# Query weights times the feature map: six heads as two row tiles of 60 rows in two PSUM banks

## The chip, the cores and the metric

The kernel runs on one core of one Trainium2 chip. The metric is the device time of one execution in microseconds; the figure quoted for a kernel is the median of several executions. TensorE multiplies matrices (a weight load and a matmul are records of their own, PEld and PE), VectorE (DVE), ScalarE (ACT) and GpSimd (POOL) work elementwise, and SyncE (SP) issues most of the DMA transfers.

## The reference

The model mixes a linear attention with learned feature maps and a SiLU feed-forward block on the same input `x` of 2048 rows by 640, with 32 heads of width 20. The change touches the query side of the attention:

```python
q, k, v = (x @ wqkv) split in 32 heads of 20
pq = einsum("bhsd,hdf->bhsf", q, w_phi)
phi_q = concat([softmax(pq), softmax(-pq)])
...
a = (phi_q (phi_k^T v) / (phi_q phi_k^T 1 + 1e-6)) @ wo
b = silu(x @ w1) @ w2
return g * a + (1 - g) * b          # g = sigmoid(sum(x * gate_w))
```

Since `pq = x @ (wq_h @ w_phi_h)` for each head, the kernel multiplies the query weights by the feature maps once, and then projects `x` with the products. Those weight products are what the change rewrites.

## The kernel before

All large products take operands split into a high and a low part, three passes for each (`PASSES`), with single-pass matmuls. The products of weights are exceptions: they take plain fp32 operands, and each of them becomes two passes on TensorE, with a weight load and a matmul record for each pass.

The work goes in stages: keys and values with the attention state, then the hidden layer of the feed-forward block by a fast scheme of seven products (`product`, line L652) for pairs of row tiles, then the queries and the attention's output, and at last the second feed-forward product (L1642). The change lies in the second half of the hidden layer, where `fuse(gi)` is put in between the products of the loop over `n` by a table `todo`: group 0 at one place of the pair `p = 1`, groups 1 and 2 in `p = 2`, 3 and 4 in `p = 3`, 5 in `p = 4`. The order on TensorE, VectorE, ScalarE and GpSimd is that of the code (`inorder`); on SP's queue a scheduler sets it.

One call of `fuse(gi)` handles a group of `GR` = 6 heads, so `GW` = 120 rows of the transposed query weights `wqT`; groups 0 to 4 are full (`NG` = 5), and group 5 has the two heads that are left, `REST` = 40 rows. It loads these rows (`wTq`), and for each of the `NC` = 5 chunks of 128 model columns multiplies the chunk (stationary, 120 rows by 128 columns) by the group's block-diagonal feature maps (moving, 120 rows by 120 columns, from `bd` in the tile `consts`). The first four chunks go to one PSUM bank (tiles `pwq..._0`), the fifth to another (`pwq..._4`). `split` then writes the high part with ScalarE and the rest with VectorE into `WQ` (tile `wq`), which is read much later, by the query projections (L519). `bank` hands out the eight PSUM banks in a fixed turn, to these products and to those of the hidden layer (tiles `p`, L652).

Other products that the prediction looks at are `pn` (L1331), which put 64 columns of weights alternately into the lower and the upper half of the array's columns.

Of the kernel before, what the change touches and what calls it, by code (L numbers as in the profile page):

```python
# [16 lines left out]
P = 128  # L17
S = 2048
D = 640
H = 32  # L20
DH = 20
F = 1728
NC = D // P
# [6 lines left out]
GR = 6  # L30
GW = GR * DH
NG = H // GR
REST = D - NG * GW
NJ = 2 * NG + 1
RC = 2 * REST
KH = 3
KD = KH * DH
# [3 lines left out]
HW = 64  # L41
C_MASK, C_EYE = 0, KF
C_ALL = C_EYE + 3 * HW
GAP = 2 * (HW - KD)
NPRE = 9
PB = (4, 5, 6, 7, 0, 1, 2, 3)
NQ = NF // 2
# [20 lines left out]
def mix_kernel(ctx: ExitStack, tc: tile.TileContext, xT, wqT, wkc, wkr, wv, bd, bdc, cst, wo, w1, w1r, w2, out):  # L68
    nc = tc.nc
# [36 lines left out]
    def raw(name):  # L106
        return rawp.tile([P, D + 2], F32, tag="raw", name=name, bufs=4)
# [10 lines left out]
    def big(name, home):  # L118
        t = big_tile(name, home)[:, : 2 * NC * D]
        return t.rearrange("p (s c d) -> p c s d", s=2, d=D)  # L120

    def wslot(name, dt=F32):
        return fq.tile([P, 2 * D], dt, tag="w", name=name, bufs=NPRE)

    def split(hi, lo, src, lo_eng="dve"):
        nc.scalar.copy(hi, src)  # L126
        eng = nc.vector if lo_eng == "dve" else nc.gpsimd
        eng.tensor_tensor(lo, src, hi.bitcast(F32), op=ALU.subtract)  # L128
# [27 lines left out]
    g = wp.tile([P, NT], F32, name="g")  # L156
# [73 lines left out]
        X["t", u].extend(t[:, :, k * 256 : (k + 1) * 256] for k in range(r.shape[1] // 256))  # L230

    def load_fused(gi, r):
        n = min(GW, D - gi * GW)
        nc.sync.dma_start(r[:n, :], wqT[gi * GW : gi * GW + n, :])

    def fused_mm(b, gi, r, c, out):
        n = min(GW, D - gi * GW)
        nc.tensor.matmul(out, r[:n, c * P : (c + 1) * P], b[:n, gi, :n], start=True, stop=True)  # L238

    def fused(b, hi, lo, gi, r, pp, c0, c1):  # L240

        n = min(GW, D - gi * GW)
        flat = pp if len(pp.shape) == 2 else pp.rearrange("p a b -> p (a b)")
        pv = flat.rearrange("p (b f) -> p b f", f=P)
        for c in range(c0, c1):
            fused_mm(b, gi, r, c, pv[:, c - c0, :n])
        cs = slice(gi * GW, gi * GW + n)
        split(hi[:, c0:c1, cs], lo[:, c0:c1, cs], pv[:, : c1 - c0, :n])

    def two(name):  # L250
        return wslot(name, F32R).rearrange("p (s d) -> p s d", s=2)
# [119 lines left out]
    for k in range(WARM):  # L371
# [4 lines left out]
            start=(k == 0),  # L376
            stop=(k == WARM - 1),
# [422 lines left out]
    with inorder(ACT, DVE, POOL, SP):  # L800
# [38 lines left out]
        t = NT - 1  # L839
# [3 lines left out]
        with inorder(PE):  # L843
# [23 lines left out]
            cs = [slice(c * 512, (c + 1) * 512) for c in range(2)]  # L867
# [79 lines left out]
    def bank(name):  # L947
        k = turns["bank"] = turns.get("bank", -1) + 1
        return ps.tile([P, 512], F32, tag=f"bank{(0, 2, 3, 4, 5, 6, 7, 1)[k % 8]}", name=name, bufs=1)
# [135 lines left out]
    kvb = {}  # L1085

    def load_b_consts():
        c = wp.tile([P, NC * WC], F32, tag="big0", name="consts", bufs=1)
        kvb["bd"] = c[:GW, : GR * P].rearrange("p (g f) -> p g f", f=P)
        kvb["cst"] = c[:, GR * P : GR * P + C_ALL - C_EYE]  # L1090
        nc.scalar.dma_start(kvb["bd"], bd)
        nc.scalar.dma_start(kvb["cst"], cst[:, C_EYE:])
        kvb["kvm"] = c[: KF + 1, 2 * D : 4 * D]
        nc.scalar.dma_start(kvb["kvm"], kv_d[: KF + 1])
# [76 lines left out]
    def fuse(gi):  # L1171
        rq = raw(f"wTq{gi}")
        load_fused(gi, rq[:, :D])
        for c0, c1 in ((0, 4), (4, NC)):
            fused(kvb["bd"], WQ[:, :, 0, :], WQ[:, :, 1, :], gi, rq, bank(f"pwq{gi}_{c0}"), c0, c1)

    def last_tables():
        kvb["zbc"] = wslot("zbc")
# [17 lines left out]
    with inorder(PE, DVE, ACT, POOL):  # L1196
# [5 lines left out]
        for n in range(1, NQ):  # L1202
            todo = plan(n)
            if n in (1, 3):
                i = n // 2
# [3 lines left out]
            if n in (2, 4):  # L1209
                i = n // 2 - 1  # L1210
# [9 lines left out]
        WQ = big("wq", 1)  # L1220
        for n in range(NQ, 2 * NQ):
            p = n - NQ
            todo = plan(n)
            if p == 0:
                todo[2] += [n_steps(1, 3)]
                todo[5] += [load_b_consts]
                todo[3] += [do(x_raw, 3, 0), do(x_raw, 3, 1)]
            if p == 1:
                todo[3] += [gates_out]
                todo[7] += [n_steps(1, 0), n_steps(1, 1)]  # L1230
            for gi in ((), (0,), (1, 2), (3, 4), (5,), ())[p]:
                todo[(4, 2)[gi % 2]] += [do(fuse, gi)]
            if p == NQ - 1:
                todo[0] += [last_tables]
                todo[1] += [lambda: w_odd_parts(kvb.pop("odd"))]
                todo[2] += [make_kvw, load_wo]
                todo[4] += [lambda: q_open(8, q_proj(8)), do(q_feat, 8)]
                todo[3] += [do(xb_load, 0)]
            h_pair(n, todo)
# [123 lines left out]
    def n_gaps(u):  # L1363
        nc.sync.dma_start(
            oTs[u][KD : KD + GAP].bitcast(F32),
            r_d[u].rearrange("(c k) s h t -> k s c (h t)", k=GAP),
        )
# [413 lines left out]
    with inorder(PE, DVE, ACT, POOL):  # L1781
# [36 lines left out]
        for b in range(1, NB):  # L1818
            acc = {k: o_acc(b, k) for k in (*KO, 0)}
            for f in range(NK):  # L1820
# [7 lines left out]
                for k in (*KO, 0) if f in (0, NC) else (1, 2, 3, 0, 6, 7, 5, 4):  # L1828
# [20 lines left out]
                    else:  # L1849
                        mh, h, with_ = {2: (0, 0, 1), 4: (1, 0, 7), 3: (0, 1, 5)}[k]  # L1850
# [90 lines left out]
```

## Time and profile before

| | |
|---|---|
| median of 3 runs | 721.98 us (721.87 to 722.0) |
| profiled execution | 721.97 us, span 720.2 us |
| TensorE busy | 714.1 us, 99% of the span, 4464 matmul records |
| VectorE, ScalarE, GpSimd busy | 530.5, 324.8, 311.4 us |
| weight products of the queries, L238 | 60 passes between 277.0 and 316.6 us |
| granted TensorE clock | 0.998 of full speed |

A row of the timeline gives the start and the length in microseconds from the span's start, the engine, the line, the operation, the tiles written and read, the rows and columns of the weights (as 120*128), the moving operand, and how many equal instructions follow each other. A length is that from the first one's start to the last one's end; a matmul's own length is longer than the step from one to the next, since they overlap. In square brackets stands the idle time of the engine ahead of the row and what ended it.

### The profile page before, as it was taken

What the parts mean: (1) busy time and instruction counts of PE and PEld (TensorE: products, weight loads), DVE (VectorE), ACT (ScalarE), POOL (GpSimd) and SP (SyncE); (2) the same over time, 40 slices, a digit from 0 to 9 for tenths busy, and PEclk for the clock granted to TensorE, in tenths of its full rate; (3) what the DMA queues carried; (4) which work ended last, traced back from release to release, by engine and by line L of the source; (5) the groups of instructions that cost most, each with busy time, mean ns of one, the idle gap of its engine ahead of it and who ended that gap; (6) DMA issues with size and microseconds to landing.
All of it is one profiled execution on the core that took longest, in us unless ns stands there. A gap on an engine that the chain in (4) does not pass through costs nothing.

```text
span 720.2 us, 12096 instructions
## 1 busy us (share of the span) xinstructions
PE 714.1 (99%) x4464; PEld 639.7 (89%) x4464; DVE 530.5 (74%) x981; ACT 324.8 (45%) x642; POOL 311.4 (43%) x223
## 2 busy tenths in 40 slices
PE   9999999999999999999999999999999999999997
PEld 7888888888888888888998999999898899999996
DVE  5677667679968996654678776767447998786975
ACT  5444344556645465535444634343424443243340
POOL 2378888894354623215557566644200000300302
PEclk9999999999999999999999999999999999999999
DMA  8232110200446487536100322011469528362622
GB/s 269 89 104 88 38 39 27 74 16 16 150 151 217 154 251 244 189 101 201 54 1 25 97 83 69 25 38 33 135 179 343 174 77 246 105 211 81 209 77 74
DMA packets 53967, 85.53 MB, mean 119 GB/s; under 512 B 5482, under 2 KB 24186, under 8 KB 53908
## 3 DMA queue, kind: packets, MB, share of 16 engines
q1 hardware_dynamic: 52213, 81.56, 35.4%
q10 hardware_dynamic: 1695, 3.20, 1.5%
q8 instruction: 35, 0.57, 0.3%
q14 instruction: 24, 0.20, 0.1%
HBM read 58.82 MB, written 25.92 MB: 118 GB/s over the span
## 4 chain that ended last, share of the span: by engine, by line
PE 94%; DVE 3%; ACT 1%; DMA 1%; POOL 0%; issue 0%; SPq 0%; DVEq 0%; ACTq 0%; POOLq 0%
PE acc L1642 25%; PE p L652 20%; PE kvp L560 17%; PE pa L1382 10%; PE pq L519 7%; PE pn L1331 2%; PE kv L530 2%; PE pT L1251 2%; PE kvp L600 2%; PE kvp L410 1%; PE kvq L410 1%; PE pwk L398 1%; PE pwq L238 1%; DVE eq L510 1%; ACT eq L1008 1%; DMA wvr<-wv 1%
## 5 line engine op out<-in xcount | busy, mean ns | idle before, releaser
L1642 PE MATMUL acc<-u,w 128*128 128x512 f32 (+1 forms) x600 | 115.6, 339 | 0.5 <-DVE acc_x L1839 0.5
L1642 PEld LDWEIGHTS acc<-u,w 128*128 128x128 f32 x600 | 95.4, 190 | 12.4 <-DVE acc_x L1839 1.0
L560 PE MATMUL kvp<-wh,xa 128*128 128x512 f32 (+1 forms) x420 | 91.6, 354 | 0.0
L1650 POOL TENSOR_TENSOR o_0l<-o_0l,y 128x512 f32<-128x512 f32 x3 | 3.9, 1291 | 183.1 <-DMA ur<-u_d 111.8
L560 PEld LDWEIGHTS kvp<-wh,xa 128*128 128x128 f32 x420 | 70.3, 188 | 10.2
L1382 PE MATMUL pa<-oT,wo 128*128 128x256 f32 x600 | 74.3, 283 | 0.0
L1382 PEld LDWEIGHTS pa<-oT,wo 128*128 128x128 f32 x600 | 72.3, 188 | 0.9 <-issue 0.7
L1022 POOL TENSOR_TENSOR ez<-eq,zbc 128x1280 f32<-128x1280 f32 x16 | 47.0, 2938 | 30.7 <-ACT eq L1008 28.8
L615 ACT ACTIVATE u<-p 128x512 f32<-128x512 f32 x47 | 28.1, 599 | 67.9 <-issue 34.5
L128 POOL TENSOR_TENSOR ph<-ek,ph 128x1280 fp32r<-128x1280 f32 x15 | 44.8, 2984 | 19.4 <-ACT ph L126 17.9
L1058 POOL TENSOR_TENSOR eq<-eq,sm 128x1280 f32<-128x1280 f32 x16 | 37.9, 2368 | 33.3 <-DVE sm L1052 29.9
L279 POOL TENSOR_TENSOR wt<-wr 128x256 f32<-128x256 f32 (+1 forms) x36 | 27.9, 775 | 51.7 <-DVE ws10b L282 10.6
L126 ACT CAST t<-ur 128x512 fp32r<-128x512 f32 x36 | 22.4, 621 | 60.5 <-DVE ur L282 58.5
L360 ACT CAST v<-kvp 128x8 fp32r<-128x8 f32 (+3 forms) x75 | 16.8, 270 | 69.4 <-PE kvp L560 63.8
L560 PE MATMUL kvp<-wl,xa 128*128 128x512 f32 (+1 forms) x210 | 47.1, 354 | 0.0
L128 DVE TENSOR_TENSOR u<-ur,u 128x512 fp32r<-128x512 f32 x52 | 38.3, 762 | 6.3 <-ACT u L126 6.3
L1642 PEld LDWEIGHTS acc<-t,s 128*128 128x128 f32 x324 | 40.9, 191 | 1.0
L1642 PE MATMUL acc<-t,s 128*128 128x256 f32 x324 | 41.7, 283 | 0.0
L560 PEld LDWEIGHTS kvp<-wl,xa 128*128 128x128 f32 x210 | 35.7, 189 | 5.5
L588 POOL TENSOR_TENSOR ek<-ek,st 128x1280 f32<-128x1280 f32 x15 | 36.1, 2404 | 9.0 <-ACT v L360 6.2
L519 PE MATMUL pq<-wq,xb 128*128 128x320 f32 x240 | 37.2, 312 | 0.0
L519 PE MATMUL pq<-wq,xn 128*128 128x320 f32 x240 | 36.8, 310 | 0.0
(467 smaller groups left out, 1652.4 us busy)
## 6 DMA issues: line engine op xcount, KB each, us to landing
u_d<-u SPq DMA_DIRECT2D x52, 256.0 KB
ur<-u_d SPq DMA_DIRECT2D x52, 256.0 KB
wr<-w SPq DMA_DIRECT2D x24, 320.0 KB
w2r<-w SPq DMA_DIRECT2D x13, 320.0 KB
y<-fb_d SPq DMA_DIRECT2D x8, 512.0 KB
xra<-xT SPq DMA_DIRECT2D x14, 256.0 KB
xr<-xT SPq DMA_DIRECT2D x14, 256.0 KB
fb_d<-pac SPq DMA_DIRECT2D x14, 256.0 KB
```

The source lines that it names most:

```text
L126: nc.scalar.copy(hi, src)
L128: eng.tensor_tensor(lo, src, hi.bitcast(F32), op=ALU.subtract)
L279: nc.gpsimd.tensor_tensor(o[k], x, y, op=op)
L519: nc.tensor.matmul(dst, xt[c][:, hx, :], w[:, c, hw, lo : lo + n], start=first, stop=(hx == 1 and c == NC - 1))
L560: nc.tensor.matmul(kv_cols(t, k, lo, hi), xt[c][:, hx, :], WKV[hw][k][:, c, lo:hi], start=(n == 0), stop=(n == 3 * NC - 1), skip_group_che ...
L588: nc.gpsimd.tensor_tensor(groups(e), groups(e), spread(st[:, 1, :]), op=ALU.mult)
L615: nc.scalar.activation(o, src, AF.Silu)
L652: nc.tensor.matmul(dst, W[n][w][:, hw, j * P : (j + 1) * P], x[:, hx, :], start=(i == 0), stop=(i == len(todo) - 1))
L1022: nc.gpsimd.tensor_tensor(ez, Q[t]["e"], kvb["zbc"], op=ALU.mult)
L1058: nc.gpsimd.tensor_tensor(groups(q["e"]), groups(q["e"]), spread(q["sm"][:, 2 * H : 4 * H]), op=ALU.mult)
L1382: nc.tensor.matmul(pa[:, a, :], kvb["wo"][:, c, hw, ds], o[:, ho, c, :], start=(k == 0), stop=(k == len(todo) - 1),)
L1642: nc.tensor.matmul(dst, lhs, rhs, start=(first and n == 0), stop=(last and n == len(todo) - 1), skip_group_check=True)
```

## The change

The 120 rows of a full group are laid out as two tiles of 60 rows, at rows 0 to 59 and 64 to 123 of 128 (`ROWS`, with four rows of zeros between, so `wqT` and `bd` grow), and each tile multiplies its three heads alone: 60 rows of weights by a moving block of 60 columns. The two tiles of a chunk follow each other in the code and write to two banks, tile 0 to `pwq..._0` and tile 1 to `pwq..._1`, five chunks of 60 columns in each. Group 5 keeps its five products of 40 rows and puts them in one bank. The copies of a full group become two of 5 x 60 columns per engine instead of 4 x 120 and 120; group 5 has one per engine instead of two.

```diff
+GP = HW + KD
+ROWS = ((0, KD), (HW, KD))
...
     def load_fused(gi, r):
-        n = min(GW, D - gi * GW)
-        nc.sync.dma_start(r[:n, :], wqT[gi * GW : gi * GW + n, :])
-
-    def fused_mm(b, gi, r, c, out):
-        n = min(GW, D - gi * GW)
-        nc.tensor.matmul(out, r[:n, c * P : (c + 1) * P], b[:n, gi, :n], start=True, stop=True)
-
-    def fused(b, hi, lo, gi, r, pp, c0, c1):
-
-        n = min(GW, D - gi * GW)
-        flat = pp if len(pp.shape) == 2 else pp.rearrange("p a b -> p (a b)")
-        pv = flat.rearrange("p (b f) -> p b f", f=P)
-        for c in range(c0, c1):
-            fused_mm(b, gi, r, c, pv[:, c - c0, :n])
-        cs = slice(gi * GW, gi * GW + n)
-        split(hi[:, c0:c1, cs], lo[:, c0:c1, cs], pv[:, : c1 - c0, :n])
+        n = GP if gi < NG else REST
+        nc.sync.dma_start(r[:n, :], wqT[gi * P : gi * P + n, :])
+
+    def fused(b, hi, lo, gi, r, banks):
+
+        views = [t[:, : NC * HW].rearrange("p (c f) -> p c f", f=HW) for t in banks]
+        tiles = ROWS if gi < NG else ((0, REST),)
+        for c in range(NC):
+            for v, (r0, w) in zip(views, tiles):
+                rows = slice(r0, r0 + w)
+                nc.tensor.matmul(v[:, c, :w], r[rows, c * P : (c + 1) * P], b[rows, gi, :w], start=True, stop=True)
+        for a, (v, (_, w)) in enumerate(zip(views, tiles)):
+            cs = slice(gi * GW + a * KD, gi * GW + a * KD + w)
+            split(hi[:, :, cs], lo[:, :, cs], v[:, :, :w])
...
-        for c0, c1 in ((0, 4), (4, NC)):
-            fused(kvb["bd"], WQ[:, :, 0, :], WQ[:, :, 1, :], gi, rq, bank(f"pwq{gi}_{c0}"), c0, c1)
+        fused(kvb["bd"], WQ[:, :, 0, :], WQ[:, :, 1, :], gi, rq, [bank(f"pwq{gi}_{k}") for k in range(2)])
```

On TensorE, at group 0, between products of the hidden layer (`p`, from the raw and summed inputs `xn`, `xt`), the order before is this:

```order
L652 MATMUL p_4_2864<-xt_2017,ws7b 128x512 x2
L652 MATMUL p_4_2864<-xn_4_2582,ws7b 128x512
L238 MATMUL pwq_0_2885<-consts,wTq_2883 128x120 x4
L238 MATMUL pwq_4_2892<-consts,wTq_2883 128x120
L652 MATMUL p_5_2896<-xt_2014,ws7b 128x512 x2
```

In its place the changed kernel has the following, of whose ten rows of L245 the first two stand here; the other eight take the two banks in turn likewise.

```order
L652 MATMUL p_4_2864<-xt_2017,ws7b 128x512 x2
L652 MATMUL p_4_2864<-xn_4_2582,ws7b 128x512
L245 MATMUL pwq_0_2885<-consts,wTq_2883 128x60
L245 MATMUL pwq_1_2886<-consts,wTq_2883 128x60
...
L652 MATMUL p_5_2901<-xt_2014,ws7b 128x512 x2
```

Five products became ten, at the same place; the second bank is written by the second product and no longer by the fifth.

On SP's queue, around the loads of groups 2 to 5 (`wTq2` to `wTq5`), stores of the hidden layer `u_d` and weight loads `wr` stand in this order before:

```order
L234 DMA wTq2_3020<-wqT 120x640
L234 DMA wTq3_3100<-wqT 120x640
L234 DMA wTq4_3152<-wqT 120x640
L616 DMA u_d_109<-u2_3_2878 128x512
L616 DMA u_d_109<-u3_3_2910 128x512
L616 DMA u_d_109<-u3_2_2925 128x512
L1132 DMA g_d_108<-gT_2930 16x128
L262 DMA wr10_2965<-w1 128x640
L263 DMA wr10_2965<-w1 128x640
L234 DMA wTq5_3229<-wqT 40x640
L616 DMA u_d_109<-u2_4_2961 128x512
```

and in the changed kernel in this:

```order
L236 DMA wTq2_3030<-wqT 124x640
L236 DMA wTq3_3115<-wqT 124x640
L616 DMA u_d_109<-u2_3_2878 128x512
L236 DMA wTq4_3172<-wqT 124x640
L616 DMA u_d_109<-u3_3_2915 128x512
L616 DMA u_d_109<-u3_2_2930 128x512
L1132 DMA g_d_108<-gT_2935 16x128
L262 DMA wr10_2970<-w1 128x640
L263 DMA wr10_2970<-w1 128x640
L616 DMA u_d_109<-u2_4_2966 128x512
L236 DMA wTq5_3254<-wqT 40x640
```

The loads of groups 4 and 5 each moved behind one store, and three later loads on the queue (`w1l`, `w1r` and the first of `wo`) did so too.

More of the change, by code (lines that the diff above doesn't have):

```diff
@@ L1088, in load_b_consts @@
         c = wp.tile([P, NC * WC], F32, tag="big0", name="consts", bufs=1)
-        kvb["bd"] = c[:GW, : GR * P].rearrange("p (g f) -> p g f", f=P)
+        kvb["bd"] = c[:GP, : GR * P].rearrange("p (g f) -> p g f", f=P)
         kvb["cst"] = c[:, GR * P : GR * P + C_ALL - C_EYE]
@@ L1872 @@
     dt = x.dtype
-    bd = np.zeros((GW, GR, P), dt)
+    bd = np.zeros((GP, GR, P), dt)
     for h in range(H):
-        r, c = (h % GR) * DH, h // GR
-        bd[r : r + DH, c, r : r + DH] = w_phi[h]
+        r, j = ROWS[h % GR // KH][0] + h % KH * DH, h % KH * DH
+        bd[r : r + DH, h // GR, j : j + DH] = w_phi[h]
     bdc = np.zeros((GW, GR * DH + GR), dt)
@@ L1889, with spaced @@
     cst = blocks.astype(dt)
+    def spaced(a):
+        out = np.zeros((*a.shape[:-2], P, a.shape[-1]), dt)
+        for i, (r0, w) in enumerate(ROWS):
+            out[..., r0 : r0 + w, :] = a[..., i * KD : i * KD + w, :]
+        return out
     def tiles(a, n):
@@ L1906 @@
         "xT": x[0].T,
-        "wqT": wqkv[:, :D].T,
+        "wqT": np.concatenate([spaced(wqkv[:, : NG * GW].T.reshape(NG, GW, D)).reshape(NG * P, D), wqkv[:, NG * GW : D].T]),
         "wkc": rows(wqkv[:, D : D + NG * GW].reshape(NC, P, NG, GW).transpose(0, 3, 2, 1).reshape(NC, GW, NG * P), P),
```

## The prediction

> **What bounds the kernel now.** I read the page's busy times and its chain first, then the list of what TensorE waited for, then line L238, which the change replaces, and at last the timeline around single groups.
>
> ```profile
> PE 714.1 (99%) x4464; PEld 639.7 (89%) x4464; DVE 530.5 (74%) x981; ACT 324.8 (45%) x642; POOL 311.4 (43%) x223
> PE 94%; DVE 3%; ACT 1%; DMA 1%; POOL 0%; issue 0%; SPq 0%; DVEq 0%; ACTq 0%; POOLq 0%
> PE warm L372 <- DVE ones L172: 1.1, 1, 1.1
> PE acc L1642 <- DVE acc_x L1839: 0.5, 1, 0.5
> PE kvp L410 <- ACT wh L126: 0.2, 1, 0.2
> ```
>
> TensorE is busy 99% of the span and makes 94% of the chain that ended last. The last three rows are all its waits: 1.8 us in sum, at the kernel's start and end. Nothing behind the changed stage waits for an engine that runs on its own clock, so a microsecond more or less of TensorE there should reach the end one for one.
>
> ```profile
> L238 PEld LDWEIGHTS pwq<-consts,wTq x60: 182/192/193, 277.0 to 316.3; 120*128 120x128 f32 x50, 40*128 40x128 f32 x10
> L238 PE MATMUL pwq<-consts,wTq x60: 266/275/300, 277.3 to 316.3; 120*128 120x120 f32 x50, 40*128 40x40 f32 x10
> 306.29 0.40 PE L652 MATMUL p<-xn,ws9b 128*128 128x512 f32 x1
> 306.52 1.27 PE L238 MATMUL pwq<-consts,wTq 120*128 120x120 f32 x10
> 307.56 0.71 PE L652 MATMUL p<-xt,ws9b 128*128 128x512 f32 x2
> 308.10 0.40 PE L652 MATMUL p<-xn,ws9b 128*128 128x512 f32 x1
> 280.47 2.21 PE L652 MATMUL p<-xn,ws7d 128*128 128x512 f32 x9
> 314.49 0.84 PE L652 MATMUL p<-xn,ws10a 128*128 128x512 f32 x3
> 315.26 1.30 PE L238 MATMUL pwq<-consts,wTq 40*128 40x40 f32 x10
> 316.49 0.50 PE L652 MATMUL p<-xt,ws10c 128*128 128x512 f32 x1
> 316.83 0.63 PE L652 MATMUL p<-xt,ws10c 128*128 128x512 f32 x2
> 306.29 1.32 PEld L238 LDWEIGHTS pwq<-consts,wTq 120*128 120x128 f32 x10
> 315.26 1.19 PEld L238 LDWEIGHTS pwq<-consts,wTq 40*128 40x128 f32 x10 [0.35 <-issue]
> ```
>
> A product of these weights is two passes, each with a load of 128 columns. That makes 10 passes per group: five groups with 120 rows and 120 moving columns, and a sixth with 40 and 40, which the change leaves as it is on TensorE. In group 4, ten passes of 0.275 us overlap into 1.27 us, so one starts every (1.27 - 0.275) / 9 = 0.111 us. In the sixth, with a third of the rows and a third of the moving columns, the loads start every (1.19 - 0.19) / 9 = 0.111 us. The step is the same, so neither moving columns nor rows set it. What the two have in common is the load of 128 columns: this stage is bound by its weight loads.
>
> **What a change of the array's shape costs.** The sixth group is the nearest row for the new form, since 60 rows like 40 occupy half of the array's rows, between neighbours of 128. A 128x512 pass of the neighbours takes (2.21 - 0.39) / 8 = 0.227 us. From 306.29 to 308.10 lie the starts of group 4 and three neighbours: 1.81 - 0.68 = 1.13 us for ten passes. From 314.49 to 316.83 lie those of the sixth group and four neighbours: 2.34 - 0.91 = 1.43 us for ten passes at the same step. The half-height group costs 0.30 us more, around its passes and not in them: its first load starts with its first pass at 315.26, while group 4's runs under the matmul before, 0.23 us ahead of its pass, and the neighbour behind starts late likewise. The Trainium skill has this as a rule (TensorEngine Tiling (Array Packing), Key Properties): a change of the tiling mode drains TensorE, a change of tile alone does not. It gives no time; by it, too, a group pays on the way in and on the way out, not between its passes, and the sum below stays.
>
> **Two tiles at once.** No row shows two row tiles side by side. The nearest are the products pn, which alternate between two halves of the array's columns:
>
> ```profile
> L1331 PEld LDWEIGHTS pn<-fT,kvw x192: 132/137/139, 373.6 to 520.2; 120*64 120x64 f32 x160, 80*64 80x64 f32 x32
> 373.62 0.14 PEld L1331 LDWEIGHTS pn<-fT,kvw 120*64 120x64 f32 x2 [0.19 <-issue]
> 373.62 2.60 PE L1331 MATMUL pn<-fT,kvw 120*64 120x256 f32 x24
> 373.62 0.44 PE L1331 MATMUL pn<-fT,kvw 120*64 120x256 f32 x2
> 373.89 0.60 PE L1331 MATMUL pn<-fT,kvw 120*64 120x256 f32 x4
> ```
>
> Two loads of 0.13 to 0.14 us fill 0.14 us together, and two matmuls fill 0.44: in column tiles loads and passes start in pairs, within 0.01 us. I take row tiles to do the same.
>
> **The change, part by part.**
> - Passes: a group goes from 10 passes to 20 (10 products of 60 rows, two passes each), alternately in the upper and the lower half. Each half has 10 loads of 128 columns. If the halves load side by side, as pn's do, a group takes 10 steps of 0.111 us as before: 0. If they load one after the other, 10 steps are added: +1.11 us. Below nothing is bounded by the step itself: loads at half the step would give -0.56. I take 0, because pn is the only row with two tiles. The second half trails by 0.01 us.
> - The moving columns halve (120 to 60): 0, because the load's step covers them already in the sixth group.
> - Shape: five groups now change it on the way in and out, each between 128-row neighbours: 5 x 0.30 = +1.5 us, and 5 x 0.01 for the trailing half. The other end of this term is 0, if the neighbours hide the drain.
> - The second bank is needed at the second product, not at the fifth, so some 0.9 us earlier. Banks turn in eights.
>
> ```profile
> 298.77 0.59 ACT L687 COPY q<-p 128x512 f32<-128x512 f32 x1
> 307.50 0.60 ACT L615 ACTIVATE u<-p 128x512 f32<-128x512 f32 x1 [3.45 <-issue]
> 308.00 0.72 ACT L126 CAST wq<-pwq 128x480 fp32r<-128x480 f32 x2
> 286.07 1.27 PE L238 MATMUL pwq<-consts,wTq 120*128 120x120 f32 x10
> 283.11 0.85 DVE L128 TENSOR_TENSOR wq<-pwq,wq 128x480 fp32r<-128x480 f32 x2 [1.57 <-ACT wq L126]
> 308.58 0.85 DVE L128 TENSOR_TENSOR wq<-pwq,wq 128x480 fp32r<-128x480 f32 x2 [0.37 <-ACT wq L126]
> 279.56 1.40 SPq L234 DMA_DIRECT2D wTq<-wqT  x3
> 282.65 4.67 SPq L616 DMA_DIRECT2D u_d<-u  x3
> 288.82 0.32 SPq L234 DMA_DIRECT2D wTq<-wqT  x1
> 289.23 0.33 SPq L616 DMA_DIRECT2D u_d<-u  x1
> ```
>
>   For group 4 (306.52) ScalarE's copy at 298.77 frees that bank, 7 us ahead. The tightest is group 1 at 286.07, freed by VectorE's pair that ends at 283.96, 2.1 us ahead. No new stall: 0.
> - Copies: 480 and 120 elements become 300 and 300, still two instructions and 600 elements on each engine (0.72 and 0.85 us together); the sixth group loses one on each. ScalarE casts group 4 at 308.00, behind its activation and after the last pass started (307.5), so passes that end 0.3 us later may move it by some 0.1 us. TensorE has no wait here to lengthen, and the banks have 2 us: 0.
> - DMA: the five loads carry 124 rows, not 120, and `bd` too. On SP's queue the loads of groups 4 and 5 move behind one store u_d each. Group 4's is the last of three at 279.56, and would go after the store at 282.65 for use at 306.5; group 5's goes from 288.82 to behind the store at 289.23, for use at 315.26. What follows on the queue (the odd weights, wo) moves by one store likewise. 20 us of cover: 0. Without it a late load would stop TensorE for as long as it is late.
>
> Sum: +1.5 + 0.05 = +1.55 us. The profiled execution took 721.97 us (span 720.2, 1.8 outside), which stands at the median of 721.98. Forecast 723.5 us, +0.2%. The measurement tells about 0.2%, or 1.44 us, from no change: the bound lies at 723.42, so the forecast is barely above it.
>
> **Rivals.**
> - The halves take turns. If row tiles share the path of the weights, ten loads are added per group: 5 x (1.11 + 0.30) = +7.1 us, 729.0. For it: L238's step is a pure load step, and nothing shows row tiles loading together. Against it: pn. A weaker form is a limit on issue: 24 loads and 24 matmuls of pn take (2.60 - 0.27) us, 0.049 us each, and 40 instructions at that pace would need 1.95 us: 5 x (0.84 + 0.30) = +5.7, 727.7. But pn is paced by its 256 columns, so the row doesn't show a limit.
> - In between, passes side by side but started strictly in the program's order: each product then costs 0.111 + 0.007 us, +0.07 a group, 723.9. I count it with the forecast.
> - Faster, or not slower: the step halves, because a half-height load ends sooner when two share the array. Then 5 x (-0.56 + 0.30) = -1.3 us, 720.7. It decides once the step falls below 0.081 us, where the loads save what the shape costs. Against it: 40 rows load at 0.111. The Trainium skill (TensorEngine Tiling (Array Packing), Theoretical Speedup) promises up to twofold for a contraction of at most 64, which would be this case; it is a speedup of streaming, and the sixth group's rows show loads in its place.
> - The shape costs nothing, or is regained: if the cost of the sixth group belongs to its 40 rows, or a later stall is filled, the time is 722.0 to 722.5. Against it: the waits list has no stall before the end.
>
> **How the numbers follow.** Forecast with its ordered variant 0.72 (723.0 to 724.2 by itself), turns or issue 0.14, halved step 0.05, no cost 0.09. The forecast and no cost hold 0.81: range 721.9 to 724.6, with the other two left out. Of the forecast I give 0.62 to times above 723.42, because the ordered variant and the trailing half only add. Slower: 0.72 x 0.62 + 0.14 = 0.59. Faster by over 0.2% needs the halved step at its lower end: 0.03. Within 0.2%: 0.38.
>
> **What would show it.** The new line's loads start in pairs, every 0.111 us, and its ten products fill 1.1 us. The gap to the 128x512 passes on both sides grows by 0.30 us per group, as the sixth group's is now. TensorE's list of waits stays at 1.8 us. If the loads follow each other at 0.111 us, the first rival holds; if a group's passes fill 0.6 us, the faster one. A new wait of TensorE for pwq's banks or for wTq would prove my zeros wrong.

## The result, and the profile after

The changed kernel takes 731.93 us (median of 4 runs, 731.7 to 734.16) where the kernel before takes 721.99 (4 runs, 721.87 to 722.08): a ratio of 1.0144, interval 1.0132 to 1.0157, slower by 9.94 us. The forecast was +1.55 and its range ended at 724.6. The profiled execution of the changed kernel took 731.70 us (span 729.9), 0.2 us under its median.

The page's busy times, the chain's shares by engine, and the list of what TensorE waited for (waits in us: sum, times, longest), all of the kernel after:

```profile
PE 718.5 (98%) x4514; PEld 641.9 (88%) x4514; DVE 529.0 (72%) x980; ACT 324.4 (44%) x641; POOL 310.5 (43%) x223
PE 82%; DVE 8%; DMA 4%; ACT 3%; issue 3%; POOL 0%; DVEq 0%; ACTq 0%; POOLq 0%
PE pwq L245 <- ACT ws8b L288: 5.5, 1, 5.5
PE warm L372 <- DVE ones L174: 1.1, 1, 1.1
...
```

One row is new: TensorE waits 5.5 us, once, at the changed line. The chain has DMA in it, 4% against 1%. The other 4.4 us show in TensorE's busy time, which grew from 714.1 to 718.5. The timeline of TensorE places both, first at group 0 and then at group 4, which the prediction showed for the kernel before:

```profile
277.06 0.39 PE L652 MATMUL p<-xn,ws7b 128*128 128x512 f32 x1
282.99 2.40 PE L245 MATMUL pwq<-consts,wTq 60*128 60x60 f32 x20 [5.55 <-ACT ws8b L288]
...
286.76 1.05 PE L652 MATMUL p<-xt,ws7b 128*128 128x512 f32 x2
287.62 0.63 PE L652 MATMUL p<-xn,ws7b 128*128 128x512 f32 x1
...
294.65 1.33 PE L245 MATMUL pwq<-consts,wTq 60*128 60x60 f32 x20
...
315.79 0.39 PE L652 MATMUL p<-xn,ws9b 128*128 128x512 f32 x1
316.11 1.33 PE L245 MATMUL pwq<-consts,wTq 60*128 60x60 f32 x20
317.37 0.73 PE L652 MATMUL p<-xt,ws9b 128*128 128x512 f32 x2
317.94 0.40 PE L652 MATMUL p<-xn,ws9b 128*128 128x512 f32 x1
```

Group 4 is as forecast: twenty passes in 1.33 us, and from 315.79 to 317.94 lie 2.15 us, less 0.68 for three neighbours 1.47, where the kernel before had 1.13. Group 0 is another thing. TensorE idles 5.55 us ahead of it, its twenty passes then take 2.40 us, and two neighbours of 128x512 behind it take 287.62 - 286.76 = 0.86 us, nearly twice their 0.45. The next rows are windows. Each gives its start and end, its length, the busy microseconds and the instructions of TensorE's matmuls, its weight loads, VectorE, ScalarE and GpSimd, then the granted clock as a share of full speed, the busy share of the DMA engines, and GB/s:

```profile
277.00:283.00 6.00, 0.45 (x3) 0.06 (x3) 4.09 (x7) 3.41 (x7) 0.00 (x0) 0.89 0.75 222
283.00:285.00 2.00, 2.00 (x20) 2.00 (x20) 1.82 (x4) 0.00 (x0) 0.38 (x1) 0.50 0.25 96
285.00:289.00 4.00, 4.00 (x14) 3.13 (x13) 0.84 (x2) 1.62 (x4) 2.93 (x5) 0.56 0.41 150
289.00:300.00 11.00, 11.00 (x64) 8.87 (x63) 5.55 (x10) 4.87 (x11) 0.00 (x0) 1.00 0.57 201
```

The clock falls to half at 281.7, still in the idle time, and is back at 288.5, so TensorE works 5.5 us at half its clock. That is the larger part of the growth of its busy time.

What was group 0 waiting for? The waits list names ScalarE's cast `ws8b`, which the product doesn't read: the list names what ended last by the profile. The changed line's own group says more, for it also holds the waiting instructions of TensorE's sequencer (their shortest, median and longest in ns, then the first and last start). The rows of ScalarE's queue give the issue of `bd`, before and after:

```profile
L245 PEldq EVENT_SEMAPHORE  x6: 51/51/9709, 273.2 to 320.9; - x6
270.84 0.34 ACTq L1091 DMA_DIRECT2D consts<-bd  x1
271.56 0.27 ACTq L1091 DMA_DIRECT2D consts<-bd  x1
```

The longest wait, 9.71 us from 273.2, ends at 282.9. It waits for two semaphores, those of group 0's `wTq` and of `bd`, and the events of these semaphores in the trace show what happened at 282.9. A transfer reports in parts:

```
transfer            rows  issued   parts  landed
before     bd       120   270.84   15     274.06 to 274.88
after      bd       124   271.56    4     281.75 to 282.90
before     wTq0     120   263.93   15     268.33 to 270.35
after      wTq0     124   263.62    4     270.33 to 270.78
before     u_d      128   268.89   16     270.80 to 272.14
after      u_d      128   268.58   16     12 by 270.65, 4 at 275.29 to 275.75
```

With 120 rows a transfer is made of 15 parts, with 128 rows of 16, and with 124 rows, which are 4 x 31, of 4. So `bd` (372 KB) took 11.3 us instead of 4.0, and it is used at 277.3. The Trainium skill states the rule (DMA: Bandwidth & Descriptors, "Why a DMA increments its semaphore by 16 and not by 1"): a transfer runs on the largest number of engines up to 16 that divides the slowest dimension on both its sides, and on SP's and ScalarE's queues on the lowest-numbered ones. The trace agrees on the number, 15, 4 and 16; the last two rows also fit the second half, since a store on 16 engines waited 4.6 us longer for just four of its parts. Which engines these are the trace doesn't name.

### The profile page after: what moved, and what is told of

The parts are those of the page before. It is cut to its first block, busy times and chain, and to the rows that moved or that the text cites. A ratio compares the mean times of both kernels' runs of the same rounds, so it can differ in the third digit from the quotient of the medians.

```text
span 729.9 us, 12193 instructions
## 1 busy us (share of the span) xinstructions
PE 718.5 (98%) x4514; PEld 641.9 (88%) x4514; DVE 529.0 (72%) x980; ACT 324.4 (44%) x641; POOL 310.5 (43%) x223
## 4 chain that ended last, share of the span: by engine, by line
PE 82%; DVE 8%; DMA 4%; ACT 3%; issue 3%; POOL 0%; DVEq 0%; ACTq 0%; POOLq 0%
PE acc L1641 25%; PE kvp L560 17%; PE pa L1381 10%; PE p L652 8%; PE pq L519 7%; DMA u_d<-u 4%; PE pn L1330 2%; PE kv L530 2%; PE pT L1250 2%; PE kvp L600 2%; PE kvp L410 1%; PE kvq L410 1%; PE pwq L245 1%; PE pwk L398 1%; DVE p L657 1%
```

## The experiments

Each is run beside the kernel before, which took 722.12 us (9 runs, 721.83 to 722.47) in the first four and 722.15 (22 runs, 721.93 to 723.01) in the others.

**All rows loaded.** The changed kernel, with 128 rows instead of 124 in both transfers:

```diff
-        n = GP if gi < NG else REST
+        n = P if gi < NG else REST
...
-        kvb["bd"] = c[:GP, : GR * P].rearrange("p (g f) -> p g f", f=P)
+        kvb["bd"] = c[:, : GR * P].rearrange("p (g f) -> p g f", f=P)
...
-    bd = np.zeros((GP, GR, P), dt)
+    bd = np.zeros((P, GR, P), dt)
```

> The changed kernel, but the loads of bd and of the five full groups' wTq carry 128 rows instead of 124 (four more rows of zeros); row tiles, banks and the order on every queue stay. Theory (the row count of the transfers): in the changed kernel each 124-row transfer posts its completion in 4 parts where a 120-row one posts 15, so it runs on fewer DMA engines, and bd lands at 282.9 us where TensorE wants it at 277.3. With 128 rows bd should land within some 4 us of its issue, TensorE should not idle at group 0, and what is left is the shape cost of groups 1 to 4 of the changed kernel, 1.475 - 1.137 = 0.34 us, five times: +1.7 us, 723.7 us. Rival 1 (the row tiles themselves, or their first use, stall group 0): 731 to 732 us as before. Rival 2 (SP's order, in which two loads and three later ones moved behind a store): also 731 to 732 us, since that order is kept.

Measured: 724.63 us (723.83 to 725.01), ratio 1.0032 (1.0021 to 1.0044). That is 0.9 us more than the theory's 723.7. Now `bd` is issued at 269.25 and landed in 16 parts by 273.13. The timeline of TensorE at group 0, where no idle time stands in brackets any more:

```profile
277.07 0.39 PE L652 MATMUL p<-xn,ws7b 128*128 128x512 f32 x1
277.38 1.33 PE L245 MATMUL pwq<-consts,wTq 60*128 60x60 f32 x20
278.64 0.73 PE L652 MATMUL p<-xt,ws7b 128*128 128x512 f32 x2
```

With four more rows of zeros 7.3 of the 9.9 us are gone. The row tiles and the order on SP's queue, which are the same in this kernel, can't have cost those.

**The kernel before, with only `bd` longer.** Four rows of zeros are added to `bd`, nothing else:

```diff
-        kvb["bd"] = c[:GW, : GR * P].rearrange("p (g f) -> p g f", f=P)
+        kvb["bd"] = c[: GW + 4, : GR * P].rearrange("p (g f) -> p g f", f=P)
...
-    bd = np.zeros((GW, GR, P), dt)
+    bd = np.zeros((GW + 4, GR, P), dt)
```

> The kernel before, with one edit: bd has four more rows of zeros and its load carries 124 rows instead of 120; products, banks, wTq and all orders are those of before. Theory: bd alone lands 9 to 11 us after its issue at 270.8, that is at 280 to 282 us, TensorE idles 3 to 5 us at group 0 and then runs some 3 us at a lower clock: 726 to 729 us. Rivals 1 and 2 (row tiles, SP's order): no change, 722.0 us.

Measured: 726.62 us (725.68 to 727.39), ratio 1.0061 (1.0046 to 1.0076). `bd` was issued at 269.96, 0.9 us earlier than expected, and landed in 4 parts from 279.01 to 279.59; TensorE idled 2.04 us and not 3 to 5. TensorE's waits, its timeline and a window of this kernel:

```profile
PE pwq L238 <- issue: 2.0, 1, 2.0
279.68 1.35 PE L238 MATMUL pwq<-consts,wTq 120*128 120x120 f32 x10 [2.04 <-issue]
280.78 1.05 PE L652 MATMUL p<-xt,ws7b 128*128 128x512 f32 x2
281.63 0.63 PE L652 MATMUL p<-xn,ws7b 128*128 128x512 f32 x1
...
290.13 1.27 PE L238 MATMUL pwq<-consts,wTq 120*128 120x120 f32 x10
283.00:289.00 6.00, 6.00 (x26) 4.77 (x25) 4.59 (x10) 2.17 (x5) 3.35 (x5) 0.89 0.73 229
```

A kernel without any row tile stops at the same place. Group 0 comes 279.68 - 277.27 = 2.41 us later than in the kernel before, but group 1 comes 290.13 - 286.07 = 4.06 later: here too the two neighbours take 0.85 us instead of 0.45. The clock is at half from 281.0 to 284.4, beginning 1.3 us after TensorE had started again, so being 2.41 us late cost another 1.65 by the clock.

**Only one of the two transfers longer.** First the loads of `wTq` with 124 rows, `bd` with 128 (the last two edits of the first experiment alone):

> The changed kernel with bd loaded as 128 rows, and wTq still as 124. Theory, in the form that only bd has no cover: the wTq loads land late too, but ahead of their use (group 0's landed at 270.8 in the changed kernel, its use is at 277), so the time is that of the version with 128 rows everywhere, 723.7 us, at most 0.5 us more. Rival form (it is the wTq loads on few engines that hold up the stores and bd behind them): bd still lands late, 726 us or more.

Measured: 727.24 us (726.74 to 727.86), ratio 1.007 (1.0055 to 1.0085), 2.6 us above the first experiment. I had thought that only `bd` lacks cover; that was too narrow. Group 0 starts 0.6 us later, when `bd` with its 16 parts is complete at 277.90. ScalarE's waits for the stores u_d (of the kernel before, the one after, the first experiment and this one) and then TensorE in this one:

```profile
ACT u L615 <- DMA u_d<-u: 14.8, 10, 3.7
ACT u L615 <- DMA u_d<-u: 22.4, 11, 3.7
ACT u L615 <- DMA u_d<-u: 13.6, 8, 3.5
ACT u L615 <- DMA u_d<-u: 22.6, 11, 4.3
PE p L652 <- ACT u L615: 1.4, 2, 1.2
277.99 1.33 PE L245 MATMUL pwq<-consts,wTq 60*128 60x60 f32 x20
292.59 0.73 PE L652 MATMUL p<-xt,ws8b 128*128 128x512 f32 x2 [1.17 <-ACT u L615]
289.00:300.00 11.00, 9.64 (x56) 7.44 (x55) 4.69 (x8) 4.28 (x10) 0.00 (x0) 1.00 0.52 178
```

With `wTq` in four parts the stores of `u` come back late, in this kernel and in the one after alike; ScalarE needs their buffers, 8 to 9 us more of waiting, and in this kernel TensorE stops twice for ScalarE, 1.4 us in sum. The window's clock stays at 1.00 after this wait of 1.2 us.

Then the other way round, `wTq` with 128 rows and `bd` with 124 (the first edit alone):

> The changed kernel with wTq loaded as 128 rows, and bd still as 124. Theory, in the form that only bd has no cover: bd lands at 280 to 283 us, and the time is 728 to 732 us, most of the changed kernel's 731.9. Rival form (the wTq loads are what holds bd up): about 724 us.

Measured: 729.43 us (729.18 to 732.27), ratio 1.0099 (1.0082 to 1.0116), 4.8 us above the first experiment. `bd` landed in 4 parts from 281.02 to 282.81. Its profiled execution is the longest of its runs, so its sizes are high; TensorE's wait, group 0 and a window of it:

```profile
PE pwq L245 <- issue: 3.0, 1, 3.0
282.90 2.05 PE L245 MATMUL pwq<-consts,wTq 60*128 60x60 f32 x20 [3.04 <-issue]
277.00:283.00 6.00, 2.96 (x15) 2.18 (x14) 0.23 (x1) 0.00 (x0) 0.00 (x0) 1.00 0.91 215
```

ScalarE does nothing between 277 and 283 (its column shows 0.00), so no cast of it released group 0. The parts add up: 2.5 (first experiment) + 2.6 (`wTq`) + 4.8 (`bd`) = 9.9 us, where the change cost 9.94. The times add up, the places don't: with `wTq` alone longer TensorE loses time at group 0 and again for ScalarE at 292, while the kernel after has no such wait and loses all of it at group 0 and by the clock behind it. So the sum doesn't show two independent costs, and how the longer `wTq` reaches the end in the kernel after stays open.

**The same rows in two transfers.** The changed kernel with each load as two of 60 rows, which are 15 x 4; no row of zeros is loaded:

```diff
-        n = GP if gi < NG else REST
-        nc.sync.dma_start(r[:n, :], wqT[gi * P : gi * P + n, :])
+        for r0, w in ROWS if gi < NG else ((0, REST),):
+            nc.sync.dma_start(r[r0 : r0 + w, :], wqT[gi * P + r0 : gi * P + r0 + w, :])
...
-        nc.scalar.dma_start(kvb["bd"], bd)
+        for r0, w in ROWS:
+            nc.scalar.dma_start(kvb["bd"][r0 : r0 + w], bd[r0 : r0 + w])
```

> The changed kernel, with bd and each full group's wTq loaded as two transfers of 60 rows (rows 0 to 59 and 64 to 123) instead of one of 124; the four rows between are not loaded and not read. It tells the row count from the amount: fewer bytes than with 128 rows, and two issues instead of one. Theory (a transfer is spread over as many engines as its row count allows, the largest divisor up to 16: 60 rows over 15, 124 over 4): bd lands by 276 us, no idling at group 0, the time within 0.5 us of the version with 128 rows, 723.5 to 724.7 us. Rival (the split into halves or the holes slow the transfers, whatever the row count): 727 us or more.

Measured: 723.86 us (10 runs, 723.34 to 724.52), ratio 1.0022 (1.0013 to 1.0031). Each half of `bd` came in 15 parts, and both were complete at 273.39. The timeline at groups 0, 1 and 4:

```profile
277.53 1.33 PE L245 MATMUL pwq<-consts,wTq 60*128 60x60 f32 x20
286.65 1.33 PE L245 MATMUL pwq<-consts,wTq 60*128 60x60 f32 x20
308.11 1.33 PE L245 MATMUL pwq<-consts,wTq 60*128 60x60 f32 x20
```

This is what the row tiles cost when the transfers run wide: +1.71 us. Against it, the kernel after has lost 282.99 - 277.53 = 5.46 us at group 0, 294.65 - 286.65 = 8.00 at group 1, and the same 8.00 at group 4; its median is 8.07 higher. So all that the rows of the transfers cost was lost between 277 and 290, 5.5 us as idle time and 2.5 us as work at the lower clock, and it went to the end one for one. The 0.8 us between this experiment and the first stay open: the groups of both traces are alike, and the intervals overlap.

**The tiles one after the other.** The first experiment's kernel with its two loops swapped, five products of the lower tile and then five of the upper:

```diff
-        for c in range(NC):
-            for v, (r0, w) in zip(views, tiles):
+        for v, (r0, w) in zip(views, tiles):
+            for c in range(NC):
```

> The version with 128-row transfers, but a group's five products of the lower half stand ahead of its five products of the upper half instead of in turn. It tells what the pairing of the halves needs. Theory (the two halves overlap because the second half's instructions stand close behind the first's): the halves run one after the other, a group takes up to 20 steps of 0.111 us instead of 10, up to 5 x 1.11 = +5.6 us over the version with 128 rows, 728 to 730 us. Rival (TensorE looks far enough ahead, past 20 records): the same as in turn, 723.8 to 724.7 us.

Measured: 728.1 us (727.98 to 728.78), ratio 1.0082 (1.0069 to 1.0096). TensorE at group 2:

```profile
294.00 0.39 PE L652 MATMUL p<-xn,ws8b 128*128 128x512 f32 x1
294.32 2.04 PE L245 MATMUL pwq<-consts,wTq 60*128 60x60 f32 x20
296.29 0.72 PE L652 MATMUL p<-xt,ws8b 128*128 128x512 f32 x2
296.86 0.40 PE L652 MATMUL p<-xn,ws8b 128*128 128x512 f32 x1
```

A group takes 2.86 - 0.68 = 2.18 us, 0.71 more than with the tiles in turn, and 5 x 0.71 = 3.5 us are the difference to the first experiment (728.10 - 724.63). So the pairing of loads is real, and it hangs on the order; but by its steps the result lies between the two expectations, with the time at the lower end of the theory's range. The single starts show six passes of the lower tile alone; the upper tile's first starts together with the lower tile's seventh, its next three come half a step behind the lower tile's last three, and six of the upper tile are left alone. With 0.71 us more, a group takes some 16.4 steps of 0.11 us, neither 10 nor 20. (The profiled execution, the longest of its runs, also has a wait of 1.4 us for ScalarE at the products `pn`.)

**Fewer changes of shape.** The first experiment's kernel, with groups 1 and 2 one behind the other, and 3 and 4:

```diff
-                todo[(4, 2)[gi % 2]] += [do(fuse, gi)]
+                todo[4] += [do(fuse, gi)]
```

> The version with 128-row transfers, but groups 1 and 2 stand right behind each other on TensorE, and so do 3 and 4; five stays of the half-height shape become three. It tells whether the 0.34 us belong to a change of shape or to a group. Theory (to the change): two of five are saved, -0.68 us against the version with 128 rows, and the second group of a pair follows the first at the step of 0.112 us. Rival (to each group's own ten products): no difference.

Measured: 724.76 us (724.34 to 725.73), ratio 1.0034 (1.0022 to 1.0046), no better than the first experiment. The trace shows the saving, and two waits of TensorE, of which the first experiment had the first with 0.2 us and the second not at all:

```profile
291.00 0.39 PE L652 MATMUL p<-xn,ws8b 128*128 128x512 f32 x1
291.32 2.44 PE L245 MATMUL pwq<-consts,wTq 60*128 60x60 f32 x40
293.70 0.73 PE L652 MATMUL p<-xt,ws8b 128*128 128x512 f32 x2
294.26 0.40 PE L652 MATMUL p<-xn,ws8b 128*128 128x512 f32 x1
PE pn L1330 <- ACT fT L1266: 1.7, 1, 1.7
PE pT L1250 <- POOL eq L1058: 1.3, 1, 1.3
```

Two groups take 3.26 - 0.68 = 2.58 us instead of 2 x 1.47: one change of shape less saves 0.36. The price per change is shown in the trace, a gain in time is not. The waits, in the queries' stage, are those of the profiled execution, the longest of this kernel's runs (725.73); whether its other runs have them I can't say. The edit also moved a load of `wTq` and some loads behind it on SP's queue by one store, so the order there isn't quite that of the first experiment.

**The sixth group at full height.** The kernel before, where group 5's 40 rows are filled up with zeros to 120 and still move 40 columns:

```diff
-        n = min(GW, D - gi * GW)
+        n = GW
...
-        nc.tensor.matmul(out, r[:n, c * P : (c + 1) * P], b[:n, gi, :n], start=True, stop=True)
+        nc.tensor.matmul(out, r[:GW, c * P : (c + 1) * P], b[:GW, gi, :n], start=True, stop=True)
```

> The kernel before, but group 5's 40 rows are padded with zeros to 120, so that its products use the whole height like those of the other groups (still 40 moving columns); its wTq load carries 120 rows. Theory (the shape's change costs 0.31 us, whatever is in the rows): group 5 takes 1.13 us instead of 1.44, the kernel is 0.3 us faster than before, 721.7 us, which the runs can hardly resolve but the trace can. Rival (the cost is that of 40 rows or 40 columns): group 5 stays at 1.44 us.

Measured: 722.22 us (11 runs, 721.65 to 722.77), ratio 0.9998 (0.999 to 1.0007). The timeline of TensorE:

```profile
314.82 1.07 PE L652 MATMUL p<-xn,ws10a 128*128 128x512 f32 x4
315.74 1.21 PE L238 MATMUL pwq<-consts,wTq 120*128 120x40 f32 x10
316.77 1.41 PE L652 MATMUL p<-xt,ws10c 128*128 128x512 f32 x5
```

The last neighbour ahead starts at 314.82 + 3 x 0.227 = 315.50, and 1.27 us later the first one behind, as around group 4 of the kernel before (306.29 to 307.56); with 40 rows it was 1.55. So the 0.3 us of the sixth group go with its height of 40 rows and not with its 40 columns. That they are paid for a change of shape, as the prediction assumed, and not for each half-height group, is what the experiment before shows, in its trace. The time can't tell 0.3 us.

## Why the prediction was wrong

- **The failed step is the DMA term.** The prediction said "the five loads carry 124 rows, not 120, and `bd` too … 20 us of cover: 0". It gave the four more rows no cost of their own, and looked for cover only for the loads that moved on SP's queue. (For those the cover held: no list has a wait of TensorE at groups 4 and 5.) The runs show +4.8 us for `bd` and +2.6 for `wTq`, 7.3 to 8.1 together. Two things were missed. The number of rows sets in how many parts a transfer runs, so each of the changed transfers fell from 15 to 4. And `bd` was put under the 20 us of groups 4 and 5, while its own cover, never worked out, was 277.27 - 274.88 = 2.4 us.
- **Its price for a late load was too low as well.** "A late load would stop TensorE for as long as it is late": group 0 came 5.46 us late, and the lower clock behind that took another 2.5.
- **The step and the pairing were right.** Two row tiles load side by side: pairs of passes start 0.007 us apart, one pair per 0.112 us. Turns at the weights' path (729.0) and a limit on issue (727.7) did not show, though their times lie nearer to the result than the forecast; the swapped loops are the only kernel in which the tiles mostly take turns, and there a group takes 2.18 us and not 1.47.
- **Shape was right in kind and nearly in size.** Forecast 5 x 0.30 + 5 x 0.01 = 1.55 us; the groups measure 5 x (1.47 - 1.13) = 1.7, and with transfers that run wide the time is 1.71 higher. The rule of the Trainium skill that was quoted there (TensorEngine Tiling (Array Packing), Key Properties) agrees: one change less saved 0.36 us, while the step between passes stayed. The twofold speed on the same page of the Trainium skill (Theoretical Speedup), which the prediction took for one of streaming though the page doesn't say of what, showed in passes alone: twenty of 60 rows fill the ten steps. It brought no time, since the kernel before needs only ten passes for the same work, and the halved moving columns don't set the step.
- **Banks and copies** at 0 were right: no list has a wait of TensorE for `pwq`'s banks.
- **A microsecond of TensorE reaches the end one for one**: right; 8.00 us at group 1 became 8.07 in the median.
- The sign that would prove the zeros wrong was named in advance as a new wait of TensorE for `pwq`'s banks or for `wTq`. A new wait came at these products, but for `bd`, which the sign didn't name.

## What to carry to other kernels

Padding a tile changes its transfers. Ask for the largest divisor up to 16 of the number of rows (120 and 60 rows ran in 15 parts, 128 in 16, 124 in 4), and work out the cover of every transfer whose shape changes, from its own landing to its own first use. These products are bound by weight loads, so splitting their rows into tiles bought nothing, and each stretch in another shape cost some 0.34 us.

## What the runs showed of the hardware

- Transfers of 124 rows came in 4 parts, of 120 and of 60 in 15, of 128 in 16. Such a transfer holds up others too: behind two loads in 4 parts, four of the sixteen parts of a store came 4.6 us after the rest.
- Idle times of TensorE of 2.04, 3.04 and 5.55 us went with 3.4, 6.8 and 6.8 us at half clock, which began between 1.3 us after the idle time's end and 1.3 us ahead of it. One of 1.17 us had none.
- Passes of two row tiles start in pairs although the code has both passes of a product ahead of those of the next; with the tiles in blocks of ten passes the upper tile's first started ahead of only the last three of the lower tile, so TensorE doesn't look far ahead.
- A change of the array's shape and back costs 0.28 to 0.36 us, with one tile of 40 rows and with two of 60.
